# Decoding staged in PSUM, block sums of x on TensorE, and g read back earlier, in a fused attention and two-layer kernel

## The chip, the cores and the metric

One core of a Trainium2 chip runs the whole program. The metric is the device time of one execution in microseconds (us). Its engines run side by side, each through its own queue in order: TensorE (PE in the profile; PEld is its weight load), VectorE (DVE), ScalarE (ACT), GpSimd (POOL) and SyncE (SP), which here issues every DMA. An instruction that waits holds up all that stands behind it on its engine.

## The reference

Inputs q, k, v and g_norm are float32; the weights come as float64. Four batches of 576 tokens, 8 heads of 64.

```python
kv  = einsum('bhsd,bhse->bhde', k, v)
out = einsum('bhsd,bhde->bhse', q, kv)
x   = out / sqrt(mean(out*out, -1) + 1e-6) * g_norm      # -> 2304 x 512
g   = (x @ w_a) * (x @ w_b)                              # 2304 x 1536
y   = g @ w_out                                          # 2304 x 512
h   = y @ w_in                                           # 2304 x 1024
solu = h * softmax(h)
ln   = (solu - mean(solu)) / sqrt(var(solu) + 1e-6) * g_ln
return ln @ w_out2                                       # 2304 x 512
```

## The kernel before

**Attention.** For each batch, four pairs of heads: `att_kv` (L651, L655) forms kv of a pair from a tile `kv` in one of two buffers, so the load of the third pair waits until TensorE has used the first. `att_1` (L681) multiplies 128 tokens of q by kv for one tile of tokens, ScalarE squares (L707), VectorE reduces (L697), GpSimd takes the power (L709), VectorE scales (L710). `att_2` (L741) transposes the result into PSUM, ScalarE copies it scaled by g_norm (L761). There are 20 such tiles.

**Operands of the first product.** x @ w_a and x @ w_b are done as seven block products (`PROD`, P1 to P7) in place of eight; they need sums of blocks of x (`t_sums`, L720 to L728: three VectorE instructions per tile) and of the weights (`sums`, L489, also three). Each operand is kept as a high and a low part: ScalarE copies the high part (`pair_ops`, L733), VectorE or GpSimd subtracts it (`tt`, L266, printed as L269). x is cut into three groups of 288, 416 and 448 columns; groups 0 and 1 (12 tiles) are summed tile by tile, group 2 (8 tiles) in `third_group` once all tiles are there, in one chain of two steps.

**Weights.** They arrive as 64-bit words. `decode` turns a chunk of 128 x 512 into two float32 parts: ScalarE (L428), then five VectorE instructions (L431, L434, L440, L445, L449) on a scratch tile `u` and a tile `f` in SBUF. For each of twelve blocks f of w_a and w_b, two chunks are decoded, added (`gather`), summed (`sums`) and split into the operand `aw` (`make_w`); there is one stage buffer (`R_ST`) and two operand slots (`R_W`). The later weights (w_out, w_in, w_out2: 28 "late" chunks) are decoded beside the products; the twelve of w_out go to HBM (`lscw`) and are read back when x's place `a01` is free (`late_loads`, L974).

**Products.** A `Set` is one f with one group: seven products of 6 matmuls each (L865) on three PSUM banks, with copies by ScalarE (L883) and sums by VectorE (L896, L917, L924, L937) and GpSimd (L939). The result g goes to HBM (L947). All eight banks are shared.

**Second half.** `g_more` (L987) reads g back in pieces of 128 x 512 (L1004) and splits them (L1013, L269); `y_run` (L1041 to L1043) multiplies by w_out; `run_h` (L1083 to L1085, the helper `three`) by w_in; softmax and statistics follow on VectorE and ScalarE; `run_t` (L1158) transposes; `run_o` (again L1083) multiplies by w_out2.

**Order.** Nothing is scheduled by hand: `Order` keeps a planned time for each engine with prices such as `t_vec` and `t_pool`, and the code emits instructions in the order of that plan. `tt` picks VectorE or GpSimd by its planned end. A changed price therefore reorders much of the program. `FIRST` says how many chunks of weights may be loaded after how many loads of the attention. `lates`, `place` and `own` decide when late chunks are loaded.

Of the kernel before, what the change touches and what calls it, by code (L numbers as in the profile page):

```python
# [17 lines left out]
P = 128  # L18
# [46 lines left out]
NOP = 7  # L65
EARLY = 2
# [12 lines left out]
class Order:  # L79
# [48 lines left out]
    def load(self, nbytes):  # L128

        self.dma = max(self.dma, self.now + 0.7) + nbytes / 360e3  # L130
        return self.dma + 1.1
# [52 lines left out]
def t_pool(n):  # L184
    return 0.22 + n * 2.2e-3
# [7 lines left out]
def attention_moe_moe_kernel(ctx: ExitStack, tc, kv_in, kv_tail, q_in, g_norm, w1, w_in, w_out2, g_ln, out):  # L193
# [42 lines left out]
    ps_free = {i: 0.0 for i in range(8)}  # L236
# [49 lines left out]
    xs_ = [att.tile([P, H * D], F32, tag=f"x{i}", name=f"x{i}") for i in range(4)]  # L286

# [27 lines left out]
    FIRST = {0: 0, 3: 1, 5: 2, 12: 3, 14: 4, 28: 5, 30: 6}  # L315
    w_loads, l_loads = list(w_chunks), list(lates)
    n_load = [0, 0]
# [36 lines left out]
    def next_chunk(limit):  # L354
# [4 lines left out]
        for k in l_loads:  # L359
            if can(R_RAW, k) and (own() and left01[0] > 4 or place(k) is not None):  # L360
                l_loads.remove(k)
                return k
# [56 lines left out]
    def decode(k):  # L419
# [4 lines left out]
        ub, fb = u.bitcast(U32), f.bitcast(U32)  # L424

        def a():

            nc.scalar.activation(out=u, in_=w[:, :, 1].bitcast(F32), func=AF.Abs)  # L428

        def b1():  # L430
            nc.vector.tensor_scalar(out=u, in0=u, scalar1=WMIN, scalar2=WMAX, op0=ALU.max, op1=ALU.min)  # L431

        def b2():
            nc.vector.tensor_scalar(  # L434
                out=ub, in0=ub, scalar1=3, scalar2=0x3FFFFFF8, op0=ALU.logical_shift_left, op1=ALU.bitwise_and
            )

        def b3():

            nc.vector.scalar_tensor_tensor(  # L440
                out=fb, in0=w[:, :, 1], scalar=0xC0000000, in1=ub, op0=ALU.bitwise_and, op1=ALU.bitwise_or
            )

        def b4():
            nc.vector.tensor_scalar(out=ub, in0=fb, scalar1=0xFF800000, scalar2=None, op0=ALU.bitwise_and)  # L445

        def b5():

            nc.vector.scalar_tensor_tensor(  # L449
                out=u, in0=w[:, :, 0], scalar=2.0 ** -52, in1=u, op0=ALU.mult, op1=ALU.mult  # L450
# [13 lines left out]
        od.chain(  # L464
            [("A", 0.62, a), ("V", 0.5, b1), ("V", 0.5, b2), ("V", 0.75, b3), ("V", 0.5, b4), ("V", 0.75, b5),
             (None, 0, freed), (None, 0, last)],
            rank=rank_of(k), t=max(od.now, when),
        )
# [20 lines left out]
    def sums(f, st, t):  # L489
# [3 lines left out]
        def s32():  # L493
            nc.vector.tensor_tensor(
                out=s[:, 2:6:3], in0=s[:, 2:5:2], in1=s[:, 0:1].to_broadcast([P, 2, 256]), op=ALU.subtract)

        def ready(t):
# [47 lines left out]
    def store(k, f, u, su, t):  # L545

        what, x, y = k
        at = place(k)
        if at is None:
            at, d = l_pair[su - 2].bitcast(F32R), dr.tile([P, 2 * CH], F32, tag=f"lsc{what}{x}_{y}", name=f"lsc{what}{x}_{y}")  # L550
            lsc[k] = d
        else:
            d = None
        hi, lo = at[:, 0:CH], at[:, CH:2 * CH]
        if what == "o":
            g = gl_sb[:, x:x + 1]
            ops = [
                tt(CH, f, f, u, ALU.add),
                ("A", 0.7, lambda: nc.scalar.activation(out=hi, in_=f, func=AF.Copy, scale=g)),
                ("V", 0.7, lambda: nc.vector.scalar_tensor_tensor(  # L560
                    out=lo, in0=f, scalar=g, in1=hi.bitcast(F32), op0=ALU.mult, op1=ALU.subtract)),
            ]
        else:
            ops = [
                ("A", 0.6, lambda: nc.scalar.copy(out=hi, in_=f)),
                tt(CH, f, f, hi.bitcast(F32), ALU.subtract),
                tt(CH, lo, f, u, ALU.add),
# [783 lines left out]
```

## Time and profile before

| what | value |
|---|---|
| median of 3 runs (lowest to highest) | 774.54 us (773.36 to 777.3) |
| profiled execution, whole | 779.11 us |
| its span, first to last instruction | 777.1 us |
| TensorE busy | 712.5 us, 92% of the span |
| VectorE / ScalarE / GpSimd busy | 503.4 / 260.2 / 287.7 us |
| mean granted clock of TensorE | 0.971 |

The last chain of work is almost wholly TensorE's own. TensorE runs at two levels, 2.4 and 1.2 GHz; PEclk 1.00 is the higher one. Four stages can be told apart by the lines that TensorE runs: attention with the first two blocks f (to about 140 us), the products of f = 2 to 11 (to 384 us), the first part of y (to about 460 us), and y, h and the output together (to the end).

### The profile page before, as it was taken

What the parts mean: (1) busy time and instruction counts of PE and PEld (TensorE: products, weight loads), DVE (VectorE), ACT (ScalarE), POOL (GpSimd) and SP (SyncE); (2) the same over time, 40 slices, a digit from 0 to 9 for tenths busy, and PEclk for the clock granted to TensorE, in tenths of its full rate; (3) what the DMA queues carried; (4) which work ended last, traced back from release to release, by engine and by line L of the source; (5) the groups of instructions that cost most, each with busy time, mean ns of one, the idle gap of its engine ahead of it and who ended that gap; (6) DMA issues with size and microseconds to landing.
All of it is one profiled execution on the core that took longest, in us unless ns stands there. A gap on an engine that the chain in (4) does not pass through costs nothing. (4 is left out here: it accounts for less than half of the span.)

```text
span 777.1 us, 9816 instructions
## 1 busy us (share of the span) xinstructions
PE 712.5 (92%) x3664; PEld 622.4 (80%) x3664; DVE 503.4 (65%) x742; ACT 260.2 (33%) x444; POOL 287.7 (37%) x259
## 2 busy tenths in 40 slices
PE   5996887899989988989798899999999998999996
PEld 4785876889989988889676687888778887898885
DVE  2799877898999989993679999500642035315560
ACT  2564443334333333322334334322222222222221
POOL 1765632444463535532355754124212321122120
PEclk9898999999999999999989999999999999999998
DMA  7755003344444434523954531214002200120001
GB/s 255 285 185 185 16 23 104 144 154 143 146 148 168 164 109 158 198 78 133 407 176 163 178 125 50 55 41 122 1 14 82 89 14 14 38 65 15 14 14 41
DMA packets 36623, 87.68 MB, mean 113 GB/s; under 512 B 4448, under 2 KB 12384, under 8 KB 36576
## 3 DMA queue, kind: packets, MB, share of 16 engines
q1 hardware_dynamic: 36576, 87.05, 32.7%
q8 instruction: 29, 0.48, 0.2%
q14 instruction: 18, 0.15, 0.1%
HBM read 61.87 MB, written 25.17 MB: 112 GB/s over the span
## 5 line engine op out<-in xcount | busy, mean ns | idle before, releaser
L865 PE MATMUL ps<-a,aw 128*128 128x288 f32 (+2 forms) x1512 | 280.5, 345 | 22.6 <-DVE t L917 12.0
L865 PEld LDWEIGHTS ps<-a,aw 128*128 128x128 f32 x1512 | 260.6, 192 | 40.1 <-DVE t L917 15.4
L269 POOL TENSOR_TENSOR gy<-mx,gy 128x512 fp32r<-128x512 f32 (+1 forms) x46 | 53.8, 1180 | 96.0 <-ACT gy L1013 92.7
L939 POOL TENSOR_TENSOR gg<-gg,t 128x288 f32<-128x288 f32 (+2 forms) x36 | 47.7, 1324 | 82.4 <-DVE gg L937 72.0
L1042 PE MATMUL ps<-gy,a 128*128 128x512 f32 (+1 forms) x192 | 70.4, 366 | 3.8 <-POOL gy L269 2.2
L1083 PE MATMUL ps<-a,aw 128*128 128x512 f32 x171 | 68.9, 403 | 4.9 <-DVE aw L1168 4.7
L1041 PE MATMUL ps<-gy,a 128*128 128x512 f32 (+1 forms) x192 | 70.2, 366 | 0.0
L1043 PE MATMUL ps<-gy,a 128*128 128x512 f32 (+1 forms) x192 | 69.7, 363 | 0.0
L883 ACT COPY gg<-ps 128x288 f32<-128x288 f32 (+2 forms) x72 | 34.5, 479 | 100.1 <-PE ps L865 89.5
L1085 PE MATMUL ps<-a,aw 128*128 128x512 f32 x171 | 67.8, 396 | 0.0
L1084 PE MATMUL ps<-a,aw 128*128 128x512 f32 x171 | 67.7, 396 | 0.0
L269 POOL TENSOR_TENSOR mx<-f,u 128x512 f32<-128x512 f32 x23 | 33.0, 1434 | 68.2 <-DVE u L449 68.2
L1129 DVE TENSOR_REDUCE mx<-ps 128x1 f32<-128x1024 f32 x18 | 22.0, 1220 | 47.1 <-PE ps L1085 46.9
L1013 ACT CAST gy<-mx 128x512 fp32r<-128x512 f32 (+1 forms) x48 | 27.1, 566 | 58.6 <-DMA mx<-gd 35.6
L1042 PEld LDWEIGHTS ps<-gy,a 128*128 128x128 f32 x192 | 36.2, 189 | 11.7 <-POOL gy L269 4.3
L1168 DVE TENSOR_TENSOR aw<-ps,aw 128x1024 fp32r<-128x1024 f32 x13 | 15.9, 1222 | 45.5 <-ACT aw L1167 45.4
L1083 PEld LDWEIGHTS ps<-a,aw 128*128 128x128 f32 x171 | 32.9, 192 | 12.6 <-DVE aw L1168 5.2
L1083 PE MATMUL ps<-a 128*128 128x512 f32 (+1 forms) x106 | 40.8, 385 | 2.4 <-DVE a L1168 2.4
L709 POOL TENSOR_TENSOR r<-r,mhalf 128x8 f32<-128x8 f32 (+1 forms) x20 | 34.7, 1749 | 17.8 <-DVE r L698 17.7
L1041 PEld LDWEIGHTS ps<-gy,a 128*128 128x128 f32 x192 | 36.2, 189 | 5.6
L1043 PEld LDWEIGHTS ps<-gy,a 128*128 128x128 f32 x192 | 36.2, 189 | 5.4
L1084 PE MATMUL ps<-a 128*128 128x512 f32 (+1 forms) x106 | 40.5, 382 | 0.0
(121 smaller groups left out, 1279.3 us busy)
## 6 DMA issues: line engine op xcount, KB each, us to landing
raw<-in_w SPq DMA_DIRECT2D x24, 512.0 KB, 3.5
mx<-gd SPq DMA_DIRECT2D x48, 256.0 KB, 3.6
kv<-in_kv SPq DMA_DIRECT2D x16, 512.0 KB, 4.3
mx<-in_w SPq DMA_DIRECT2D x12, 512.0 KB, 3.4
lscw<-mx SPq DMA_DIRECT2D x12, 512.0 KB, 2.9
a<-lscw SPq DMA_DIRECT2D x12, 512.0 KB, 10.8
gd<-gg SPq DMA_DIRECT2D x12, 448.0 KB, 2.6
gd<-gg SPq DMA_DIRECT2D x12, 416.0 KB, 2.6
```

The source lines that it names most:

```text
L269: lambda e=e: e.tensor_tensor(out=out, in0=in0, in1=in1, op=op) for e in (nc.vector, nc.gpsimd)))
L709: ("G", 1.75, lambda: nc.gpsimd.tensor_tensor(out=r[0:n], in0=r[0:n], in1=mhalf[0:n], op=ALU.pow)),
L865: nc.tensor.matmul(o, lhsT=a[:, k], rhs=b[:, kt], start=first and kt == m == 0, stop=kt == 1 and m == 2, skip_group_check=not first,)
L883: od.chain([("A", t_act(s.n, True), lambda: nc.scalar.copy(out=dst(), in_=ps)), (None, 0, done)], t=t)
L939: ("G", t_pool(s.n), lambda: nc.gpsimd.tensor_tensor(out=d, in0=d, in1=t3, op=ALU.mult)),
L1013: ("A", t_act(n), lambda t=t, gh=gh: nc.scalar.copy(out=gh, in_=t)),
L1041: nc.tensor.matmul(o, lhsT=wh[:, s], rhs=gh, start=f == 0, stop=False)
L1042: nc.tensor.matmul(o, lhsT=wh[:, s], rhs=gl, start=False, stop=False)
L1043: nc.tensor.matmul(o, lhsT=wl[:, s], rhs=gh, start=False, stop=f == NF1 - 1)
L1083: nc.tensor.matmul(o, lhsT=ah, rhs=bh, start=first, stop=False)
L1084: nc.tensor.matmul(o, lhsT=ah, rhs=bl, start=False, stop=False)
L1085: nc.tensor.matmul(o, lhsT=al, rhs=bh, start=False, stop=last)
```

## The change

- The scratch tile of decoding lies in PSUM banks 6 and 7 (`v = pst[:, 6 + su]`) for chunks in the first two buffers; the sets and y have the other six banks until the last late chunk is decoded.
- For groups 0 and 1, TensorE forms the block sums: `x` as the stationary operand times a matrix `mix` of 0, 1 and -1, four matmuls per tile into a second bank. ScalarE writes the high parts straight from PSUM, VectorE the low parts, in three instructions. `t_sums` and the tile `xs` are gone for these 12 tiles.
- `third_group` runs its sums in two chains of two quarter steps.
- `sums` of the weights may go to GpSimd; prices of `tt`, `t_pool`, `load` and the decode steps are raised.
- `g_more` loads pieces of g without waiting for a place for the split; the reads of `lscw` come block by block; eleven late chunks, not twelve, are decoded beside the products.
- A late chunk's high part is copied before its last decode step. y takes its operand slot at the end of a block, not at its start. Batch 1's kv comes after all tiles of batch 0; `FIRST` loads weights later; while tiles of attention are left only one set is active.

```diff
-    ps_free = {i: 0.0 for i in range(8)}
+    ps_free = {i: 0.0 if i < 6 else INF for i in range(8)}
...
-        return ("VG", (t_vec(n), t_pool(n)), tuple(
+        return ("VG", (0.2 + n * 1.3e-3, t_pool(n)), tuple(
...
+    mix = {}
+    for n in (P, D):
+        c = n // 2
+        m1, m2 = (att.tile([P, 4, c], F32, tag=f"m{n}_{i}", name=f"m{n}_{i}") for i in range(2))
...
-    FIRST = {0: 0, 3: 1, 5: 2, 12: 3, 14: 4, 28: 5, 30: 6}
+    FIRST = {0: 0, 6: 1, 9: 2, 14: 3, 16: 4, 28: 5, 30: 6}
...
-        ub, fb = u.bitcast(U32), f.bitcast(U32)
+        v = pst[:, 6 + su] if su < 2 else u
+        vb, fb = v.bitcast(U32), f.bitcast(U32)
...
-            nc.vector.tensor_scalar(out=u, in0=u, scalar1=WMIN, scalar2=WMAX, op0=ALU.max, op1=ALU.min)
+            nc.vector.tensor_scalar(out=v, in0=v, scalar1=WMIN, scalar2=WMAX, op0=ALU.max, op1=ALU.min)
...
-            ("V", t_vec(256), lambda: nc.vector.tensor_tensor(out=s[:, 4], in0=s[:, 2], in1=s[:, 3], op=ALU.add)),
-            ("V", t_vec(512), s32),
-            ("V", t_vec(256), lambda: nc.vector.tensor_tensor(out=s[:, 6], in0=s[:, 1], in1=s[:, 5], op=ALU.subtract)),
+            tt(256, s[:, 4], s[:, 2], s[:, 3], ALU.add),
+            tt(512, s[:, 2:6:3], s[:, 2:5:2], s[:, 0:1].to_broadcast([P, 2, 256]), ALU.subtract),
+            tt(256, s[:, 6], s[:, 1], s[:, 5], ALU.subtract),
...
-            if 0 < i and b < B - 1:
+            if 0 < b < B - 1 and i:
                 front.append(("kv", b + 1, i - 1))
+        if not b:
+            front += [("kv", 1, p) for p in range(NP)]
...
+        for kt in range(2):
+            o = pt[:, kt * 4 * c:(kt + 1) * 4 * c]
+            for first, m in ((True, m1), (False, m2)):
+                p = kt if first else kt + 2
+                nc.tensor.matmul(o, lhsT=x[0:n, p * P:(p + 1) * P], rhs=m[0:n], start=first, stop=not first)
...
-            ops += t_sums(s, full[:, 8:16]) + pair_ops(hi, lo, full[:, 2:16]) + [(None, 0, done2)]
...
-                at = place(k)
+                at = place(k) if k[0] != "w" or k[1] < 2 or len(g_q) < len(YB) * NF1 and k[1] < y_next[1] + 6 else None
...
-        while g_q and R_GI.ok() and R_GP.ok():
+        while g_q and R_GI.ok():
...
-        if not now and order and len(sets) < ACTIVE:
+        if not now and order and len(sets) < (1 if att_left[0] else ACTIVE):
```

What this moves shows in the order of instructions at three places. The first is TensorE's queue at the first tiles of attention. `kv` and `tail` feed `att_kv`; `bd` with `q` is `att_1`; `ident` with `x` is the transpose of `att_2`; `m` is the new matrix. Before:

```order
L681 MATMUL ps<-bd_0_100,q_0_157 128x128
L681 MATMUL ps<-bd_1_102,q_1_159 128x128
L681 MATMUL ps<-bd_2_104,q_2_161 128x128
L681 MATMUL ps<-bd_3_106,q_3_163 128x128
L741 MATMUL ps<-ident,x_120 128x128 x4
L651 MATMUL ps<-kv_2_224 128x128 x4
L655 MATMUL ps<-tail_0_185 128x128
```

With the change:

```order
L723 MATMUL ps<-bd_0_100,q_0_176 128x128
L723 MATMUL ps<-bd_1_102,q_1_179 128x128
L723 MATMUL ps<-bd_2_104,q_2_181 128x128
L723 MATMUL ps<-bd_3_106,q_3_183 128x128
L785 MATMUL ps<-ident,x_120 128x2x64 x4
L809 MATMUL ps<-m_0_124,x_120 128x256
L809 MATMUL ps<-m_1_125,x_120 128x256
```

Behind the transposes now stand the new matmuls of the same tile (these two twice, then the next tile); the kv pairs of batch 1, which stood between the tiles of batch 0, come after them.

The second place is SP's queue where the products of groups 0 and 1 are done and those of group 2 still run. `a<-lscw` reads w_out back, `mx<-gd` reads g, `raw` is a chunk of weights. Before:

```order
L974 DMA a_81<-lscw_2_2621 128x1024
L974 DMA a_81<-lscw_2_2777 128x1024
L1004 DMA mx<-gd_82 128x512
L1004 DMA mx<-gd_83 128x512
L1004 DMA mx<-gd_84 128x512
L947 DMA gd_93<-gg_1_2840 128x2x416
L334 DMA raw_125<-in_w_out 128x512
```

With the change:

```order
L352 DMA raw_146<-in_w_out 128x512
L1036 DMA a_81<-lscw_2_1155 128x1024
L1036 DMA a_81<-lscw_2_1306 128x1024
L1062 DMA mx<-gd_82 128x512
L1062 DMA mx<-gd_83 128x512
L1062 DMA mx<-gd_84 128x512
L1036 DMA a_81<-lscw_2_1484 128x1024
```

The first three pieces of g stood behind all twelve reads of w_out; now they stand behind two of them.

The third place is TensorE's queue at the last tile: `ident,mx` is the transpose of `run_t`, and what follows it is `run_o`. Before:

```order
L1084 MATMUL ps<-aw,a_81 128x512
L1085 MATMUL ps<-aw,a_81 128x512
L1158 MATMUL ps<-ident,mx 128x128 x8
L1083 MATMUL ps<-a_81 128x256
L1084 MATMUL ps<-a_81 128x256
```

With the change:

```order
L1153 MATMUL ps<-aw,a_81 128x512
L1154 MATMUL ps<-aw,a_81 128x512
L1227 MATMUL ps<-ident,mx 128x128 x16
L1152 MATMUL ps<-a_81 128x512
L1153 MATMUL ps<-a_81 128x512
```

The output product of the last tile (in halves of 256) followed its own transpose at once; now two transposes stand together, and the output product of the tile before (512 wide) stands between the last transpose and its product.

## Rows read from the trace of the kernel before

**Rows 1.** Busy time by stretch: start:end, length, then engines, clock, DMA, GB/s.
```profile
0.00:50.00 50.00, 37.93 (x225) 32.00 (x226) 30.94 (x70) 23.09 (x51) 22.47 (x21) 0.93 0.75 263
50.00:104.00 54.00, 45.07 (x309) 41.35 (x309) 44.67 (x84) 29.40 (x55) 29.68 (x18) 0.94 0.26 90
104.00:140.00 36.00, 27.18 (x123) 23.56 (x121) 28.55 (x38) 11.38 (x16) 12.96 (x7) 0.95 0.23 81
140.00:345.00 205.00, 194.47 (x1078) 183.89 (x1078) 187.35 (x292) 73.83 (x134) 93.04 (x65) 0.98 0.42 146
345.00:384.00 39.00, 35.58 (x181) 32.70 (x180) 23.18 (x36) 10.79 (x19) 10.77 (x8) 0.96 0.64 243
384.00:460.00 76.00, 66.58 (x270) 52.05 (x271) 63.99 (x75) 29.98 (x49) 46.06 (x31) 0.96 0.52 184
460.00:777.00 317.00, 305.69 (x1484) 256.85 (x1482) 124.66 (x152) 81.75 (x123) 72.68 (x111) 0.98 0.15 42
```

**Rows 2.** TensorE's waits: line, waited for, us in total, times, longest.
```profile
PE ps L865 <- DVE t L917: 12.0, 10, 2.4
...
PE ps L741 <- DVE xs L724: 5.7, 1, 5.7
PE ps L1083 <- DVE aw L1168: 4.7, 2, 2.4
...
PE ps L865 <- DVE aw L269: 3.1, 2, 2.6
PE ps L1041 <- ACT a L1013: 3.0, 1, 3.0
PE ps L865 <- ACT t L883: 2.8, 3, 1.5
...
PE ps L865 <- ACT a L733: 2.4, 1, 2.4
PE ps L1083 <- DVE a L1168: 2.4, 1, 2.4
```

**Rows 3.** Timeline of TensorE in attention: start, us, line, count of records.
```profile
28.88 1.06 PE L651 MATMUL ps<-kv 128*128 128x128 f32 x8
29.87 0.48 PE L655 MATMUL ps<-tail 64*128 64x128 f32 x2
```

**Rows 4.** DMA issues: tile, count, KB each, median us to landing.
```profile
kv<-in_kv SPq DMA_DIRECT2D x16, 512.0 KB, 4.3
...
q<-in_q SPq DMA_DIRECT2D x16, 288.0 KB, 5.4
```

**Rows 5.** Timelines of GpSimd and VectorE at 55 us.
```profile
55.67 2.20 POOL L269 TENSOR_TENSOR a<-xs,a 128x896 fp32r<-128x896 f32 x1 [2.82 <-ACT a L733]
...
55.83 2.33 DVE L431 TENSOR_SCALAR u<-u 128x512 f32<-128x512 f32 x1
```

**Rows 6.** Single lines of VectorE: duration ns min/median/max, first and last start.
```profile
L431 DVE TENSOR_SCALAR u<-u x40: 413/420/2327, 11.5 to 470.1; 128x512 f32<-128x512 f32 x40
...
L440 DVE SCALAR_TENSOR_TENSOR f<-raw,u x40: 674/692/1787, 12.5 to 474.4; 128x512 uint32<-128x512 uint32 x40
...
L710 DVE TENSOR_TENSOR x<-ps,r x20: 672/683/693, 25.4 to 98.5; 128x512 f32<-128x512 f32 x16, 64x512 f32<-64x512 f32 x4
```

**Rows 7.** VectorE's groups at 170 to 340 us: count, busy us, mean ns, idle.
```profile
L494 DVE TENSOR_TENSOR mx<-mx 128x512 f32<-128x512 f32 x7 | 6.7, 963 | 0.1
...
L504 DVE TENSOR_TENSOR mx<-mx 128x256 f32<-128x256 f32 x7 | 6.6, 938 | 0.0
...
L502 DVE TENSOR_TENSOR mx<-mx 128x256 f32<-128x256 f32 x7 | 4.0, 569 | 0.0
```

**Rows 8.** Timeline of TensorE in the products, between two waits.
```profile
250.09 22.39 PE L865 MATMUL ps<-a,aw 128*128 128x416 f32 x126 [0.54 <-DVE t L917]
```

**Rows 9.** Timeline of SP's DMA queue ahead of y.
```profile
363.85 9.53 SPq L974 DMA_DIRECT2D a<-lscw  x12
...
375.66 2.86 SPq L1004 DMA_DIRECT2D mx<-gd  x3
```

**Rows 10.** A stretch behind one of the three L1083 waits, columns as Rows 1.
```profile
565.00:570.00 5.00, 5.00 (x16) 3.99 (x17) 3.18 (x5) 0.00 (x0) 1.51 (x3) 0.69 0.00 0
```

More of the change, by code (lines that the diff above doesn't have):

```diff
@@ L359, in next_chunk @@
         for k in l_loads:
-            if can(R_RAW, k) and (own() and left01[0] > 4 or place(k) is not None):
+            if can(R_RAW, k) and (own() and n_late[0] < IN_AB or place(k) is not None):
                 l_loads.remove(k)
+                n_late[0] += 1
                 return k
@@ L462, in last @@
                 gather(k, f, u, su, t)
[L464 to L468, printed above, removed]
+        ops = [("A", 0.67, a), ("V", 0.68, b1), ("V", 0.68, b2), ("V", 0.7, b3), ("V", 0.6, b4), ("V", 0.7, b5),
+               (None, 0, freed), (None, 0, last)]
+        if is_late(k) and k[0] != "o":
+            ops[5:5] = [(None, 0, lambda t: upper(k, f, su, t))]
+        od.chain(ops, rank=rank_of(k), t=max(od.now, when))
     def gather(k, f, u, su, t):
@@ L563, in store @@
         else:
[L564 to L567, printed above, removed]
-            ]
+            ops = [tt(CH, lo, f, u, ALU.add)]
         def done(t):
@@ L745, in att_2, with scaled @@
         rank = 1 + b
-        if g == 2:
-            sxs = None
-            s = g2s[:, :, c0:c0 + c]
-        else:
-            sxs = R_XS.take()
-            full = att.tile([P, 16 * 64], F32, tag="xs", name=f"xs{b}_{t}", bufs=2)
-            full = full[:, 0:16 * c].rearrange("p (r c) -> p r c", c=c)
-            s = full[:, 0:8]
+        if g < 2:
+            R_PA.take()
+        def scaled(out, src, m):
+            return ("A", t_act(m, True, True), lambda: nc.scalar.activation(
+                out=out, in_=src, func=AF.Copy, scale=gn[:, 0:1]))
@@ L774, in att_2 @@
-        od.chain(ops, rank=rank, t=od.now + 0.25)
+        if g == 2:
+            R_X.give(sx)
+            od.chain([scaled(g2s[:, :, c0:c0 + c], rows, 8 * c), ps_done(bank), (None, 0, done),
+                      (None, 0, lambda t: one_left(g, t))], rank=rank, t=od.now + 0.25)
+            return
+        bank2, pt = ps_tile()
+        m1, m2 = mix[n]
+        for kt in range(2):
[3 more added lines that the diff above has]
+                nc.tensor.matmul(o, lhsT=x[0:n, p * P:(p + 1) * P], rhs=m[0:n], start=first, stop=not first)
@@ new lines, in att_2, with done2 @@
+        R_X.give(sx)
+        hi, lo = (y[:, :, c0:c0 + c] for y in x_ops(g))
+        left = [2]
+        def done2(when):
+            R_PA.give(1)
+            left[0] -= 1
+            if not left[0]:
+                one_left(g, when)
+        sums = pt[:, 0:8 * c].rearrange("c (k r t) -> c k r t", k=2, r=4)
+        for bk, src, h, l, m, dt in (
+            (bank, rows[:, 2:8], hi[:, 0:6], lo[:, 0:6], 6 * c, 0.25),
+            (bank2, None, hi[:, 6:14], lo[:, 6:14], 8 * c, 1.2),
+        ):
+            if src is None:
+                h, l = (y.rearrange("p (r k) c -> p k r c", k=2) for y in (h, l))
+                low = [("V", t_vec(m // 2, True), lambda k=k, h=h, l=l: nc.vector.scalar_tensor_tensor(
+                    out=l[:, k], in0=sums[:, k], scalar=gn[:, 0:1], in1=h[:, k].bitcast(F32),
+                    op0=ALU.mult, op1=ALU.subtract)) for k in range(2)]
+                src = sums
+            else:
+                low = [("V", t_vec(m, True), lambda src=src, h=h, l=l: nc.vector.scalar_tensor_tensor(
+                    out=l, in0=src, scalar=gn[:, 0:1], in1=h.bitcast(F32), op0=ALU.mult, op1=ALU.subtract))]
+            od.chain([scaled(h, src, m)] + low + [ps_done(bk), (None, 0, done2)], rank=rank, t=od.now + dt)
@@ L790, in third_group @@
         slot = R_ST.take()
-        full = wst.rearrange("p (r c) -> p r c", c=GN[2] // 2)
-        step = GN[2] // 2
-        left, left_b = [4], [2]
+        left, left_b = [6], [2]
         def done(t):
@@ L1026, in y_can @@
         if f == 0:
-            t = max(t, ps_ready2(2)) if R_Y.ok() else INF
+            t = max(t, ps_ready2(2))
+        if f == NF1 - 1 and not R_Y.ok():
+            return INF
         return t
@@ L1044, in y_run @@
         end = od.now + 12 * t_mm(n)
-        od.chain([(None, 0, lambda t: R_GP.give(sg)), (None, 0, lambda t: g_more())], t=end)
+        od.chain([(None, 0, lambda t: R_GP.give(sg)), (None, 0, lambda t: g_split())], t=end)
         y_next[1] += 1
```

142 lines of the change are left out of this document (82 added, 60 removed).

## The prediction

> **What bounds the kernel now.** I read the busy time by stretch first, then TensorE's list of waits, then single rows. TensorE is busy 92% of the span, so a gain has to come out of its gaps and its slow clock, and every matmul added costs unless it fills a gap. The stretches [rows 1] show where the gaps are. Up to 140 us TensorE is busy 37.9 of 50, 45.1 of 54 and 27.2 of 36 us: 29.8 us idle, and the granted clock of 0.93, 0.94 and 0.95 says that about 3.5 + 3.2 + 1.8 = 8.5 us more went at the lower level. From 140 to 345 us it idles 10.5 us (clock 0.98, 4 us), while VectorE is busy 187 of 205 us: two engines are nearly full. From 345 to 384 us 3.4 us are idle, from 384 to 460 us 9.4 us (clock 0.96, 3 us). After that only 11.3 us are idle, 4 of them behind the last matmul.
>
> The list of waits [rows 2] names VectorE for most of it. The largest, 12.0 us in ten waits, is the sum in line 917: it waits in VectorE's queue behind decoding. In the attention stage 5.7 us (sums of x), 2.4 us (split of group 2) and 2.6 us (split of weights) are the long ones. The last stage has three waits of 2.4 us each for line 1168, each where a tile's output product follows its transpose at once.
>
> Why VectorE is so full shows in two rows: GpSimd's subtraction takes 2.20 us from 55.67 us on, and a step of decoding beside it takes 2.33 us [rows 5], against a median of 0.42 us [rows 6]. Line 440 ranges from 0.67 to 1.79 us. Line 710, which reads PSUM, ran 20 times between 0.67 and 0.69 us beside the same GpSimd work [rows 6]. So operands in SBUF are stretched by GpSimd and those in PSUM were not.
>
> **The change part by part.** I sum against the profiled execution, 779.1 us (span 777.1 and 2 us around it), which is 4.6 us over the median.
>
> *Attention and the first two weight blocks (0 to 140 us).* The four added matmuls per tile are 256 columns wide for ten tiles and 128 for two. Eight records in line 651 are four matmuls of 128 columns in 1.06 us [rows 3], 0.265 us each. A 256-column one lies between that and double, 0.53 us; I take 0.47, near the upper end, since the columns are streamed. 40 x 0.47 + 8 x 0.265 = 21 us (12.7 to 23.3) on the bounding engine. What they replace, per tile, is three sums on VectorE, a subtraction of the low part on VectorE or GpSimd and a copy on ScalarE; three low parts from PSUM come to VectorE, at line 710's rate (0.683 us for 512 columns) 0.5 + 0.34 + 0.34 us. The clash with GpSimd leaves this path, and the 5.7 us wait for `xs` has no cause left. Of the 29.8 us idle and 8.5 us slow clock, the waits for VectorE and for group 2 and the slow clock behind them are about 21 us; I take 18 as filled, since the third group's two halves run on two engines at once and TensorE has products left meanwhile.
>
> Two new waits come with the order. kv has two buffers, so batch 1's third pair is loaded only after TensorE has used the first; in between stands one pair, (1.06 + 0.48) = 1.5 us, and a load lands after 4.3 us [rows 3, 4]: 2.8 us of wait. Behind that load on SP stand the fourth pair, a chunk of weights and all q of batch 1 (5.4 us to land [rows 4]), so the first tile of batch 1 waits about as long: 5.6 us together. Before, tiles stood between those pairs. The weights' chunks are issued behind q; the first set needs all of batch 0's tiles anyway, which hides that. One chunk fewer stands ahead of batch 0's q: 0.5 MB at 263 GB/s [rows 1] is 2 us gained. Sum: 21 - 18 + 5.6 - 2 = +6 us, between -4 (matmuls at 0.27, all 21 filled) and +14 (12 filled).
>
> *Products of f = 2 to 11.* Decoding a chunk on VectorE is three steps of 0.42 and two of 0.69 us undisturbed, 2.64; in PSUM I bound the step from both sides by 0.42 and 0.69 and take 0.69 (line 710's row is PSUM), 3.45 us. Disturbed, the stage pays more than 2.64: the sums of weights in the same stage average 0.96, 0.94 and 0.57 us [rows 7], 2.47 per f. Of these 36 instructions 29 now stand on GpSimd. At 2.20 us for 896 columns [rows 5] it needs 2.5 us per f for them and is busy only 93 of 205 us. So VectorE loses some 2 us per f out of 21 and gains slack; the waits for line 917 should fall. What is there to win is the stage's 10.5 + 4 us and, to 384 us, 3.4 + 1.6. Against it: with six banks and one set active at some ends of f, P4 follows P7 at once in two more places (about 0.65 us each, as in two of the three waits for line 883 [rows 2]), and the weights' chain (decode, gather, sums, copy, split, through one stage buffer) has the sums on the slower engine. TensorE's floor per f is 22.4 us for 126 matmuls [rows 8]; before, an f took about 23.2 us. I take 8 us of the 19.5, -18 to +3.
>
> The Trainium skill, "VectorE: DVE Perf Modes", section "Why PSUM operands drop a tier", says that a float32 instruction with a PSUM operand runs one element per cycle. That speaks against the change: three of the five steps lose their double rate. "SBUF — State Buffer", section "Who interferes with whom", says that an instruction with at most one SBUF input outside those modes doesn't contend with GpSimd. By the first alone the products gain 4 us, by both 8.
>
> *Start of y.* The three pieces of g stood behind 9.5 us of w_out reads [rows 9]; now behind two of twelve. The 3.0 us wait [rows 2] and the slow clock behind it (3 us) go; the later 6.4 us of waits are for splits, whose loads now run ahead: 12.4 at most. The other ten reads are asked for six blocks ahead of use (12 matmuls of 0.24 us a block, worked out below, is 17 us), which hides them. Two costs: y's second block needs a pair of banks of the first block while 6 and 7 hold decoding (0 to 2.6 us, I take 1), and sixteen late chunks cost VectorE 0.8 us more each undisturbed where it is already busy 64 of 76 us (I take 3). Net -8 (-12 to 0).
>
> *The last stage.* In the new order another product stands between every transpose and its output product. The waits of 2.4 + 2.4 + 2.4 us go, and the slow clock behind each: 0.69, 0.66 and 0.66 over 5 us (the first is [rows 10]), 5 us. Left: the last transpose now has only one output product and a transpose ahead (24 matmuls of 512 columns at 22.39/126 x 512/384 = 0.24 us each, and 0.9 us), and the product behind it waits for its own drain, up to 2.4 less 0.9 us; I take 2. -10 (-12 to -7).
>
> Part with one answer: the matrices of 0 and 1 are made while TensorE waits for the first kv.
>
> **The rivals.** *Attention costs nothing and the products reach their floor.* VectorE's relief decides both: 0 - 15 - 11 - 11 = -37, 742 us in the trace, 737 as a median. For it: VectorE is named in most waits. Against: a wait for DMA isn't VectorE's.
>
> *The weights' chain binds.* GpSimd's sums take away what PSUM gives: products 0, attention +10, y -7, end -10, that is -7: 767. For it: VectorE's other work on SBUF is still stretched by a busier GpSimd [rows 5].
>
> *Slower.* The same chain gets longer than the products' time: with period T per f in place of 23.2 us the nine f that wait for it cost 9 x (T - 23.2); the other terms give 12 us (6 - 8 - 10), so it decides from T = 24.5 on, and at T = 26 the end is 13 us over: 787. GpSimd takes over 29 instructions that are each slower than on VectorE, and a set's multiplication (L939) queues with them.
>
> *It doesn't do what it says: PSUM only slows decoding.* Steps at 0.69 us and the two that read `raw` still stretched: products -4, y 0 since VectorE is full there (64 + 16 x 0.8 = 77 of 76 us), end -10, attention +6: -8, 766. The page on perf modes, cited above, is the rule by which this would come; the trace bears it out as far as the 0.42 against 0.69 us goes, and speaks against the stretching.
>
> **How the numbers follow.** 6 - 8 - 8 - 10 = -20: 759.1 in the profiled execution, less 4.6 gives a median of 754 us, -2.6%. Chances: the forecast 0.48 (744 to 764); attention free and products at the floor 0.18; chain binds 0.18 (760 to 775); slower 0.08; PSUM only slows 0.08. The range of 8 in 10 runs from 737 to 771: half of the best rival lies below, most of the slower case and a part of the chain's above. A measurement here tells about 0.5% (3.9 us) from no change: faster 0.86 (all but a third of the chain's case and the slower one), same 0.08, slower 0.06.
>
> **What would show it.** Attention: products of f = 2 begin near 146 us (140 before), VectorE less busy ahead of it, a wait for kv's third pair of batch 1 near 38 us. Products: VectorE's decode steps within 0.67 to 0.70 us, waits for the c22 sum under 8 us, and a period of f below 23 us. y: no wait over 1 us at its first piece and a clock of 1.00 there. End: no wait for a drain behind a transpose but at the last tile. I am wrong if GpSimd appears as releaser of the weights' split, if f = 2 begins past 155 us, or if decode steps in PSUM vary.

## The result and the profile after

The changed kernel took 756.55 us (median of 4 runs, 755.03 to 757.83), the kernel before 775.92 us beside it (773.36 to 778.2): a ratio of 0.975, 95% interval 0.971 to 0.979. The prediction was 754.0 (737 to 771). The profiled execution took 757.83 us, its span is 755.9.

Three landmarks divide both executions: where the products of f = 2 begin, where the products end, and the end. These are the stretches between them, the last one cut once more at 480 us. Columns: stretch, its length, busy time of each engine with the number of instructions, granted clock, share of DMA, GB/s. Before:

```profile
core 0: us, PE busy (x) PEld busy (x) DVE busy (x) ACT busy (x) POOL busy (x), PEclk, DMA share, GB/s
0.00:140.36 140.36, 110.18 (x655) 96.90 (x655) 104.53 (x192) 63.88 (x120) 65.11 (x45) 0.94 0.43 149
140.36:383.65 243.29, 230.05 (x1258) 216.59 (x1258) 209.82 (x325) 84.62 (x153) 103.81 (x72) 0.98 0.45 162
383.65:480.00 96.35, 86.48 (x361) 68.45 (x361) 83.53 (x102) 38.76 (x62) 56.74 (x41) 0.96 0.45 160
480.00:777.00 297.00, 285.78 (x1394) 240.45 (x1392) 105.47 (x126) 72.97 (x110) 61.99 (x101) 0.98 0.15 40
```

After:

```profile
0.00:147.61 147.61, 131.69 (x750) 117.60 (x751) 100.15 (x198) 62.21 (x123) 68.01 (x53) 0.95 0.40 143
147.61:383.41 235.80, 226.15 (x1259) 213.94 (x1259) 200.73 (x296) 82.74 (x152) 122.29 (x95) 0.99 0.45 156
383.41:480.00 96.59, 91.87 (x404) 74.66 (x403) 81.92 (x115) 41.05 (x66) 53.76 (x46) 1.00 0.54 183
480.00:756.00 276.00, 270.28 (x1350) 228.82 (x1348) 103.12 (x120) 70.44 (x105) 58.67 (x96) 1.00 0.15 40
```

The first stretch is 7.25 us longer: TensorE has 21.5 us more to do there, and its idle time falls from 30.2 to 15.9 us. The products are 7.5 us shorter. From their end to the end of the span it was 393.45 us and is now 372.5, which is 21 us less, half of it idle time (21 to 10 us), half of it clock. From TensorE's list of waits after:

```profile
PE ps L926 <- POOL aw L270: 7.9, 3, 3.8
PE ps L693 <- DMA kv<-in_kv: 5.5, 2, 4.1
...
PE ps L723 <- DMA q<-in_q: 1.9, 2, 1.0
PE ps L1111 <- POOL a L270: 1.8, 2, 0.9
PE ps L1110 <- DVE aw L1136: 1.4, 1, 1.4
...
PE ps L1152 <- DVE a L1237: 1.3, 1, 1.3
...
PE ps L926 <- DVE t L978: 0.6, 1, 0.6
```

The last row is the sum that took 12.0 us in [rows 2]. The three waits of 2.4 us behind drains have shrunk to one of 1.3. At the head of the list stands a new one: the split of the weights on GpSimd. The decode steps with scratch in PSUM, by form (busy time, mean ns):

```profile
L451 DVE TENSOR_SCALAR ps<-ps 128x512 f32<-128x512 f32 x41 | 27.6, 688 | 18.2 <-ACT ps L448 18.2
L454 DVE TENSOR_SCALAR ps<-ps 128x512 uint32<-128x512 uint32 x41 | 27.9, 691 | 0.4
L460 DVE SCALAR_TENSOR_TENSOR f<-raw,ps 128x512 uint32<-128x512 uint32 x41 | 27.7, 678 | 0.7
L465 DVE TENSOR_SCALAR ps<-f 128x512 uint32<-128x512 uint32 x41 | 28.0, 686 | 0.4
L469 DVE SCALAR_TENSOR_TENSOR u<-raw,ps 128x512 f32<-128x512 uint32 x41 | 27.7, 679 | 0.4
```

None of these is under 0.63 or over 0.70 us, where [rows 6] had 0.41 to 2.33. Eleven of the 52 chunks use another buffer, whose scratch stays in SBUF, and there a step varies as before in the same execution (shortest, median and longest in ns, then first and last start):

```profile
L465 DVE TENSOR_SCALAR mx<-mx x11: 414/742/2652, 145.2 to 325.5; 128x512 uint32<-128x512 uint32 x11
```

### The profile page after: what moved, and what is told of

It is laid out like the page before. It is cut to its first block, busy times and chain, and to the rows that moved or that the text cites. A ratio compares the mean times of both kernels' runs of the same rounds, so it can differ in the third digit from the quotient of the medians.

```text
span 755.9 us, 10032 instructions
## 1 busy us (share of the span) xinstructions
PE 720.0 (95%) x3760; PEld 635.0 (84%) x3760; DVE 485.9 (64%) x726; ACT 256.4 (34%) x446; POOL 302.7 (40%) x287
## 4 chain that ended last, share of the span: by engine, by line
PE 79%; DVE 9%; DMA 3%; POOL 3%; issue 2%; ACT 2%; SPq 0%; POOLq 0%; DVEq 0%; ACTq 0%
PE ps L926 26%; PE ps L1152 9%; PE ps L1154 9%; PE ps L1153 9%; PE ps L1110 5%; PE ps L1111 5%; PE ps L1112 5%; PE ps L809 3%; PE ps L723 3%; PE ps L693 2%; PE ps L1227 2%; PE ps L785 1%; POOL mx L270 1%; DVE mx L460 1%; DMA kv<-in_kv 1%
## 5 line engine op out<-in xcount | busy, mean ns | idle before, releaser
L926 PE MATMUL ps<-a,aw 128*128 128x288 f32 (+2 forms) x1512 | 274.3, 341 | 14.7 <-POOL aw L270 7.9
L926 PEld LDWEIGHTS ps<-a,aw 128*128 128x128 f32 x1512 | 256.6, 189 | 30.2 <-POOL aw L270 8.6
L270 POOL TENSOR_TENSOR gy<-mx,gy 128x512 fp32r<-128x512 f32 (+1 forms) x43 | 50.0, 1163 | 96.4 <-ACT gy L1081 93.0
L1152 PE MATMUL ps<-a,aw 128*128 128x512 f32 (+1 forms) x178 | 67.9, 381 | 0.0
L1153 PE MATMUL ps<-a,aw 128*128 128x512 f32 (+1 forms) x178 | 67.8, 381 | 0.0
L1154 PE MATMUL ps<-a,aw 128*128 128x512 f32 (+1 forms) x178 | 67.8, 381 | 0.0
L1000 POOL TENSOR_TENSOR gg<-gg,t 128x288 f32<-128x288 f32 (+2 forms) x36 | 41.4, 1150 | 58.0 <-DVE gg L998 57.9
L270 POOL TENSOR_TENSOR mx<-mx 128x512 f32<-128x512 f32 (+2 forms) x45 | 57.7, 1287 | 6.5 <-DVE mx L270 2.0
L1237 DVE TENSOR_TENSOR aw<-ps,aw 128x1024 fp32r<-128x1024 f32 x13 | 15.9, 1224 | 44.3 <-ACT aw L1236 44.2
L1199 ACT ACTIVATE mx<-ps,mx 128x1024 f32<-128x1024 f32 x18 | 20.1, 1118 | 69.0 <-DVE mx L1198 69.0
L1152 PE MATMUL ps<-a 128*128 128x512 f32 x99 | 38.8, 392 | 1.3 <-DVE a L1237 1.3
```

Source lines behind the costliest of these rows:

```text
L926: nc.tensor.matmul(o, lhsT=a[:, k], rhs=b[:, kt], start=first and kt == m == 0, stop=kt == 1 and m == 2, skip_group_check=not first,)
L1000: ("G", t_pool(s.n), lambda: nc.gpsimd.tensor_tensor(out=d, in0=d, in1=t3, op=ALU.mult)),
L1152: nc.tensor.matmul(o, lhsT=ah, rhs=bh, start=first, stop=False)
L1153: nc.tensor.matmul(o, lhsT=ah, rhs=bl, start=False, stop=False)
L1154: nc.tensor.matmul(o, lhsT=al, rhs=bh, start=False, stop=last)
```

## The experiments

All twelve in one table, each with its median, its ratio to the kernel before beside it, and the three stretches of its profiled execution (to f = 2; products; from the products' end to the end). "After" and "before" stand for the whole change and none of it. The stretches are those of one execution each, and that one lay up to 3.2 us from the median (3.2 above it before, 1.3 above it after, 2.3 below it with scratch in SBUF), so a difference of 2 or 3 us between two kernels can be chance.

| kernel | median us | ratio (95%) | first | products | rest |
|---|---|---|---|---|---|
| before | 775.9 | 1 | 140.4 | 243.3 | 393.5 |
| after | 756.55 | 0.975 (0.971 to 0.979) | 147.6 | 235.8 | 372.5 |
| after, scratch in SBUF | 774.08 | 0.998 (0.995 to 1.001) | 145.3 | 244.2 | 380.4 |
| the same with eight banks | 766.65 | 0.988 (0.982 to 0.994) | 147.2 | 243.7 | 376.2 |
| after, slot taken early | 781.44 | 1.005 (1.002 to 1.008) | 144.6 | 238.1 | 396.1 |
| after, g late | 771.47 | 0.992 (0.989 to 0.995) | 146.7 | 238.3 | 385.3 |
| after, third group in one chain | 759.07 | 0.979 (0.974 to 0.984) | 147.2 | 239.1 | 372.6 |
| after, half of the block sums | 749.8 | 0.967 (0.962 to 0.973) | 136.2 | 238.8 | 372.6 |
| after, weight sums on VectorE | 754.96 | 0.974 (0.968 to 0.980) | 146.1 | 233.9 | 372.6 |
| after, weight split on VectorE | 755.17 | 0.974 (0.969 to 0.979) | 145.4 | 234.2 | 372.8 |
| after, third buffer for kv | 764.8 | 0.984 (0.979 to 0.989) | 146.7 | 244.7 | 373.1 |
| before with PSUM alone | 783.25 | 1.009 (1.006 to 1.011) | 142.7 | 238.7 | 397.6 |
| before with late slot alone | 770.1 | 0.993 (0.991 to 0.995) | 138.3 | 243.2 | 386.4 |
| before with both | 764.16 | 0.986 (0.980 to 0.992) | 142.0 | 238.6 | 380.2 |

**Scratch in SBUF, banks still closed.**

```diff
-        v = pst[:, 6 + su] if su < 2 else u
+        v = u
```

> The third group's decode scratch goes back to SBUF, banks 6 and 7 stay closed to the products, nothing else is changed, so every engine has the instructions of the changed kernel in the same order. Theory (the prediction's: in SBUF the decode step is stretched by GpSimd, in PSUM it isn't): decode steps of 256 columns spread again from 0.42 us to over 2 us, with means at or over the 0.68 to 0.69 us that they take in PSUM, and 759 to 766 us, 3 to 9 over the changed kernel. Rival (reading PSUM is what costs VectorE its speed, and the rest of the change carries the gain): the mean step falls clearly under 0.68 us and the time is 748 to 755 us.

(The edit puts back the scratch of the first two decode buffers, whatever the group, and the steps have 512 columns.) It took 774.08 us: nearly the whole gain is gone, about twice the most that the theory gave. The rival is out. The steps of decoding, in the same order of instructions as after:

```profile
L451 DVE TENSOR_SCALAR u<-u 128x512 f32<-128x512 f32 x41 | 27.2, 678 | 19.7 <-ACT u L448 19.7
L454 DVE TENSOR_SCALAR u<-u 128x512 uint32<-128x512 uint32 x41 | 28.3, 700 | 0.4
L460 DVE SCALAR_TENSOR_TENSOR f<-raw,u 128x512 uint32<-128x512 uint32 x41 | 39.0, 954 | 0.7
L465 DVE TENSOR_SCALAR u<-f 128x512 uint32<-128x512 uint32 x41 | 23.1, 565 | 0.4
L469 DVE SCALAR_TENSOR_TENSOR u<-raw,u 128x512 f32<-128x512 uint32 x41 | 30.6, 750 | 0.4
```

Three of the five have a median of 0.42 us, as the first of them has in [rows 6], and yet two of those three have about the mean that they have in PSUM, since single ones last up to 1.5 us. The five sum to 148.2 us here and 138.9 in PSUM; VectorE's whole busy time is 498.7 and 485.9 us. About as much is won on the other side: GpSimd is busy 314.8 us here and 302.7 after. One of its groups, after and then here:

```profile
L270 POOL TENSOR_TENSOR f<-f,a 128x512 f32<-128x512 f32 x9 | 11.7, 1295 | 16.9 <-ACT a L583 12.0 <-DVE ps L465 4.8
```

```profile
L270 POOL TENSOR_TENSOR f<-f,a 128x512 f32<-128x512 f32 x9 | 14.2, 1576 | 21.0 <-ACT a L583 18.2 <-DVE u L465 2.8
```

The stretching goes both ways, and PSUM takes it off these steps of both engines. I had priced VectorE's side alone. Decoding also ends earlier with the slower step. The last of the five, after and then here:

```profile
L469 DVE SCALAR_TENSOR_TENSOR u<-raw,ps x41: 633/678/689, 21.4 to 482.7; 128x512 f32<-128x512 uint32 x41
L469 DVE SCALAR_TENSOR_TENSOR u<-raw,u x41: 640/683/1773, 21.3 to 496.1; 128x512 f32<-128x512 uint32 x41
```

By stretch the products lose 8.4 us and the rest 7.9, while the first stretch is 2.3 shorter. In the products TensorE's idle time is 13.65 against 9.65 us, and its busy time is 4.4 us longer for the same matmuls, which is clock (0.97 against 0.99). In the rest the waits for the split of one piece of g (3.6 in place of 0.9 us), which on GpSimd stands behind late decoding, and for closed banks (2.7 and 3.0 us in place of 1.4) add up.

**The same with all eight banks open.**

```diff
-    ps_free = {i: 0.0 if i < 6 else INF for i in range(8)}
+    ps_free = {i: 0.0 for i in range(8)}
...
-        v = pst[:, 6 + su] if su < 2 else u
+        v = u
...
-                ps_free[6] = ps_free[7] = t
+                pass
```

> As the run with scratch in SBUF, and all eight banks are open to the products again, so the order may shift a little. Theory: as there, less what the two closed banks cost; that is the wait of 1.4 us of y's second block, so 757 to 766 us, within 3 us of the run with six banks. Rival (the closed banks are what the PSUM staging really costs): 5 us or more under the run with six banks, and below the changed kernel.

It took 766.65 us, 7.4 less than with six banks, which is more than the theory's 3 and what the rival asked for, but still 10 above the changed kernel, which it did not. The two profiled executions lie only 2.8 us apart, so the traces account for a part of the 7.4. With SBUF scratch the two banks matter, since decoding ends late and they stay closed until then: the waits of 2.7 and 3.0 us are gone here. After, where decoding ends earlier, the closed banks cost the one wait of 1.4 us shown above.

**Slot taken early.** y takes its operand slot at the start of a block, as before.

```diff
-            t = max(t, ps_ready2(2))
-        if f == NF1 - 1 and not R_Y.ok():
-            return INF
+            t = max(t, ps_ready2(2)) if R_Y.ok() else INF
...
+            y_op[j] = (R_Y.take(),)
...
-            slot = R_Y.take()
+            slot = y_op[j][0]
```

> y takes its operand slot at the start of a block again, as in the kernel before, and not at its end. Theory (the late taking is what lets the products of the last blocks of y run past the drains, and with it the three waits of 2.4 us behind drains went): they come back and the time is 761 to 769 us. Rival (the waits at the end went because the new plan orders the drains otherwise, and the slot is not what it turns on): the end is unchanged and the time is 755 to 758 us.

781.44 us: all of the gain is gone and more, above the theory's 769. Four rows of TensorE's timeline say why (start, us, instruction, idle time before it and its releaser):

```profile
482.01 0.77 PE L1151 MATMUL ps<-a,aw 128*128 128x512 f32 x1 [11.59 <-DVE u L469]
...
566.99 0.50 PE L1151 MATMUL ps<-a,aw 128*128 128x512 f32 x1 [2.36 <-DVE aw L1236]
...
649.37 0.50 PE L1151 MATMUL ps<-a,aw 128*128 128x512 f32 x1 [2.36 <-DVE aw L1236]
...
758.09 0.50 PE L1151 MATMUL ps<-a 128*128 128x512 f32 x1 [2.36 <-DVE a L1236]
```

The first is the first output product. The program puts it behind the decoding of the last late chunk and gives it one of decoding's two banks. The releaser, a decode step that starts at 481.2 us, shares nothing with it but that bank, so the wait is for a bank of decoding's. The program has nothing else for TensorE there: y's next block may not start, since both operand slots are held. Behind the wait the clock is 0.86 from 475 to 520 us. In the changed kernel the last decode step is as late (482.7 us), but there stand 72 matmuls of y's next block behind the first transpose, some 16 us of work (0.227 us each, by their starts). The waits behind drains come back too, with no block of y put between.

**g late.** The first pieces of g are read behind w_out again. The edit undoes three things at once: the early reads of g, the reads of `lscw` block by block, and the limit of eleven late chunks.

```diff
-IN_AB = 11
+IN_AB = 99
...
-            if can(R_RAW, k) and (own() and n_late[0] < IN_AB or place(k) is not None):
+            if can(R_RAW, k) and (own() and left01[0] > 4 or place(k) is not None):
...
-                at = place(k) if k[0] != "w" or k[1] < 2 or len(g_q) < len(YB) * NF1 and k[1] < y_next[1] + 6 else None
+                at = place(k)
...
-        while g_q and R_GI.ok():
+        while g_q and R_GI.ok() and R_GP.ok() and len(g_in) == 0 and (g_q[0][0] == 0 or gy):
```

> The first pieces of g are read behind all of w_out's reads again, and the split of g is queued as before; the rest is the changed kernel. Theory (the early pieces are what took the wait and the half clock from the start of y): y begins with a wait of 2 to 4 us and at a clock under 0.9, and the time is 760 to 765 us. Rival (the faster decoding alone had made the chain of w_out early enough): no wait over 1 us at y's first piece and 755 to 758 us.

Neither came. y starts well, with a wait of 0.69 us and a clock of 1.00 from 384 to 430 us, so the early pieces are not what took the wait from its start. But the time is 771.47 us: the rest is 12.8 us longer, and it is lost late:

```profile
710.38 1.09 PE L1227 MATMUL ps<-ident,mx 128*128 128x128 f32 x8 [1.10 <-DVE mx L1203]
...
742.04 1.09 PE L1227 MATMUL ps<-ident,mx 128*128 128x128 f32 x8 [1.98 <-DVE mx L1203]
746.60 0.79 PE L1152 MATMUL ps<-a 128*128 128x512 f32 x1 [3.46 <-DVE a L1237]
758.11 0.39 PE L1152 MATMUL ps<-a 128*128 128x256 f32 x1 [2.36 <-DVE a L1237]
```

Here y's last matmuls start at 691.8 us (684.1 after), and in TensorE's queue the last four transposes have 24, 96 and 24 matmuls between them, where after the last six, of which the first two and the last two stand together, have 72, 72 and 48. From 745 us on the clock is 0.78. So the three count together, through y's blocks being done sooner and the order of the end that follows; which of them does it isn't separated.

**Half of the block sums.** Of each pair of new matmuls the second is left out, so the combined blocks of x lack their second signed part.

```diff
-            for first, m in ((True, m1), (False, m2)):
+            for first, m in ((True, m1),):
...
-                nc.tensor.matmul(o, lhsT=x[0:n, p * P:(p + 1) * P], rhs=m[0:n], start=first, stop=not first)
+                nc.tensor.matmul(o, lhsT=x[0:n, p * P:(p + 1) * P], rhs=m[0:n], start=True, stop=True)
```

> Of the sums of x's blocks on TensorE the second matmul of each pair is left out, so the combined blocks hold only the first of their two signed parts (this part of the computation is left out): 8 pairs of 128x256 matmuls less one half. As the trace of the changed kernel has them (0.47 us each at 256 columns, 0.265 at 128) half of the added 21 us is gone. Theory (in the attention TensorE is the bound, so the added matmuls count in full): f=2 begins 7 to 11 us earlier and the time is 746 to 750 us. Rival (the first blocks of weights, not TensorE, set when f=2 begins): f=2 begins 0 to 3 us earlier and the time is 753 to 757 us.

f = 2 begins 11.4 us earlier for 10.5 us of matmuls less, so the rival is out. That they count in full is in part luck: the clock from 40 to 50 us is 0.83 here and 0.50 in the changed kernel, so TensorE's busy time falls by 15.9 us, while its idle time rises by 4.5. Then 3.0 us are given back in the products, and the median falls by 6.75.

**Third group in one chain of two steps.**

```diff
-        left, left_b = [6], [2]
+        left, left_b = [4], [2]
...
-        step = GN[2] // 4
-        for h in range(2):
+        step = GN[2] // 2
+        for h in range(1):
```

> The third group's sums in one chain of two steps in place of two chains; the rest is the changed kernel, and the order of the last stage is the same. Theory (two chains let two engines work at once on the group that is needed last): operands of the third group come 2 to 4 us later, f=2 begins up to 4 us later, 757 to 761 us. Rival (in the changed kernel the group is ready with time to spare): f=2 begins within 1 us of 147.6 and the time is 755 to 758 us.

759.07 us (757.75 to 760.91), hardly to be told from 756.55. f = 2 begins at 147.23 us, so two chains gain nothing there. Of the 3.3 us in the products 2.6 are busy time, which is clock: 0.86 against 0.93 from 140 to 165 us and 0.93 against 1.00 from 340 to 365 us, behind waits of the same length (3.66 and 3.19 us here, 3.83 and 3.22 after).

**Weight sums on VectorE, and weight split on VectorE.** Two runs, each with one of them.

```diff
-            tt(256, s[:, 4], s[:, 2], s[:, 3], ALU.add),
+            ('V', 0.53, lambda: nc.vector.tensor_tensor(out=s[:, 4], in0=s[:, 2], in1=s[:, 3], op=ALU.add)),
...
-                    tt(n, lo[:, s], x, hi[:, s].bitcast(F32), ALU.subtract),
+                    ("V", t_vec(n), lambda s=s, x=x, hi=hi, lo=lo: nc.vector.tensor_tensor(out=lo[:, s], in0=x, in1=hi[:, s].bitcast(F32), op=ALU.subtract)),
```

(The other two sums are written the same way.)

> The three kinds of weight sums are put on VectorE alone (in the changed kernel GpSimd takes most of them); their order against the rest is left to the plan. Theory (GpSimd's slow sums, not VectorE, are what makes weight operands late): no wait of TensorE for a GpSimd split or sum, 750 to 755 us. Rival (VectorE, busy for 0.91 of the products, has no room for them): TensorE waits for VectorE in the products, f rises over 23 us, and the time is 757 to 768 us.

> The split of the combined weights' low part is always put on VectorE; in the changed kernel three of TensorE's waits, 7.9 us in sum (3.83, 3.22 and 0.83), end with that split on GpSimd. Theory (GpSimd is late for it, VectorE would not be): the three waits shrink to under 3 us and the time is 749 to 754 us. Rival (the sums before the split are late on either engine, so only the last link is shorter, and VectorE's queue is as full): the waits stay over 6 us in sum, 755 to 760 us.

754.96 us (754.32 to 756.5) and 755.17 us (754.25 to 757.62): both a little under the changed kernel, with ranges that overlap. So GpSimd's share of the sums gains nothing here. With the sums on VectorE the time lies where the theory had it, but its condition did not come: the waits for GpSimd's split are 9.2 us in sum. With the split on VectorE the wait stays, under another name:

```profile
PE ps L926 <- DVE aw L549: 8.6, 3, 4.3
```

The chain ahead of it is what is late. GpSimd in the changed kernel, ahead of the wait that ends at 147.61 us:

```profile
138.53 2.55 POOL L270 TENSOR_TENSOR mx<-f,u 128x512 f32<-128x512 f32 x2 [6.42 <-DVE u L469]
141.15 0.81 POOL L270 TENSOR_TENSOR mx<-mx 128x256 f32<-128x256 f32 x1
141.97 1.29 POOL L1000 TENSOR_TENSOR gg<-gg,t 128x448 f32<-128x448 f32 x1
143.89 0.72 POOL L270 TENSOR_TENSOR mx<-mx 128x256 f32<-128x256 f32 x1 [0.62 <-DVE mx L270]
144.57 1.58 POOL L1000 TENSOR_TENSOR gg<-gg,t 128x448 f32<-128x448 f32 x1
146.11 1.45 POOL L270 TENSOR_TENSOR aw<-mx,aw 128x512 fp32r<-128x512 f32 x1
```

From the last decode step (138.5 us) to the operand it is 9 us, one instruction after the other, with two multiplications of other sets in between. No single one of them makes up the wait.

**Third buffer for kv.**

```diff
-    R_KV, R_TAIL, R_Q, R_RAW = Ring(2), Ring(1), Ring(8), Slots(3)
+    R_KV, R_TAIL, R_Q, R_RAW = Ring(3), Ring(1), Ring(8), Slots(3)
```

(and `bufs=3` for the tile)

> A third buffer for the pairs of k and v, so that the third pair of the second batch is read without waiting for the first to be used. In the changed kernel TensorE waits 1.5 us for it at 39.75 us and 4.1 us at the start, and its clock is 0.50 of full from 40 to 50 us, which costs some 5 us. Theory (the wait and the half clock behind it go together): the clock of 40 to 50 us is over 0.9, f=2 begins 4 to 6 us earlier, and the time is 750 to 753 us. Rival (the clock falls there for the loosely filled attention as such): the wait goes, the clock stays near 0.5, and the time is 755 to 757 us.

The wait of 1.5 us at 39.75 us goes, and 8 us are lost: 764.8 us. The clock from 40 to 50 us is 0.66 after three short waits for q (0.50 in the changed kernel), so that wait isn't its whole cause; what is stays open. The loss lies in the products, 8.9 us. The plan has moved work between VectorE and GpSimd (497.8 and 292.6 us busy, 485.9 and 302.7 after), and the wait for f = 11's weights is 5.7 in place of 3.2 us.

**The two large parts alone, in the kernel before.** First PSUM staging with its prices and closed banks:

```diff
+        v = pst[:, 6 + su] if su < 2 else u
...
-    ps_free = {i: 0.0 for i in range(8)}
+    ps_free = {i: 0.0 if i < 6 else INF for i in range(8)}
...
-            [("A", 0.62, a), ("V", 0.5, b1), ("V", 0.5, b2), ("V", 0.75, b3), ("V", 0.5, b4), ("V", 0.75, b5),
+            [("A", 0.67, a), ("V", 0.68, b1), ("V", 0.68, b2), ("V", 0.7, b3), ("V", 0.6, b4), ("V", 0.7, b5),
```

> The kernel before with one part of the change alone: the decode scratch of its first two buffers in banks 6 and 7, those banks closed to the products, and the plan's prices of the decode steps set as in the changed kernel. With the scratch put back in SBUF the changed kernel took 774.1 us, 18 over the changed kernel, more than the 3 to 9 expected. Theory now (staging in PSUM is worth 10 to 18 us by itself, because it takes the clash with GpSimd off both engines): 758 to 766 us. Rival (it is worth that much only in the changed kernel, whose plan was fitted to it, and the other parts would be worth as much alone): 768 to 778 us.

Neither theory nor rival: 783.25 us, slower than before. The products are 4.6 us shorter, but the first stretch is 2.3 and the rest 4.2 longer, with this in it:

```profile
482.84 0.77 PE L1086 MATMUL ps<-a,aw 128*128 128x512 f32 x1 [9.13 <-DVE u L450]
```

It is the wait that the early slot made in the changed kernel: the first output product on a bank of decoding's. It ends with the last decode step on that bank; the last step of all starts later, at 486.5 us. So the slot alone, and then both:

```diff
-            t = max(t, ps_ready2(2)) if R_Y.ok() else INF
+            t = max(t, ps_ready2(2))
+        if f == NF1 - 1 and not R_Y.ok():
+            return INF
...
-            y_op[j] = (R_Y.take(),)
...
-            slot = y_op[j][0]
+            slot = R_Y.take()
```

> The kernel before with the late taking of y's operand slot alone. Taking it early again in the changed kernel brought back four waits of 2.36 us behind drains and a wait of 11.6 us for the decoding of w_out, 23.5 us from the start of y on. In the kernel before w_out isn't waited for, so only the drains can be won. Theory (the slot frees the order of the last stage): two of the three waits of 2.36 us go with the slow clock behind them, the one at the end stays, 766 to 771 us against 777. Rival (the slot is worth nothing without the rest): 774 to 779 us.

> The kernel before with two parts: decoding staged in PSUM (with the two banks closed) and the late taking of y's slot. PSUM alone took 783 us, with a wait of 9.1 us for w_out's decoding at 482.8 us and three of 2.36 us. Theory (the two parts need each other: PSUM makes the products shorter and w_out later, and the slot gives TensorE blocks of y to do until w_out is there): the 9.1 us wait goes with 5 us of slow clock behind it, as do two of the waits behind drains with theirs, and the time is 758 to 765 us, under the sum of the two parts alone. Rival (their effects just add up): PSUM's +5 to +8 and the slot's own gain, 771 to 777 us.

The slot alone: 770.1 us, as the theory had it, and of the three waits behind drains one is left. Both: 764.16 us, as the theory had it too; the wait of 9.13 us is gone, and the products are again 4.6 us shorter than with the slot alone. The ratios are 1.009 and 0.993 alone, which would multiply to 1.001, and 0.986 together.

## Why the prediction was right, and where it was not

**The sum.** By stretch it was 6 - 8 - 18 = -20, and the traces say 7.25 - 7.5 - 21.0 = -21.2. The terms came out; several of the reasons behind them did not. The median fell by 19.4 us. The step from trace to median, -4.6, was too large: the profiled execution lay 3.2 us over the median of the four runs of the kernel before, and 1.3 over that of the changed one.

**Attention, +6: right in the price of the matmuls, in part luck in the rest.** The 256-column matmul was taken at 0.47 us, and eight records, four matmuls, last 1.89 us:

```profile
25.84 1.89 PE L809 MATMUL ps<-m,x 128*128 128x256 f32 x8
```

TensorE's busy time rises by 21.5 us where 21 were summed, and 14.3 us of gaps are filled where 18 less 5.6 of new waits plus 2 made 14.4. But the 18 counted on slow clock as well, and of that hardly any was won: the clock of the stretch is 0.94 before and 0.95 after. The new waits came smaller, kv's at 39.75 us with 1.5 in place of 2.8 us and all waits for q with 1.9; in their place 5 us went where the sum had no term, at half clock behind the wait for kv (stretch, length, TensorE's busy time, its clock, DMA share and GB/s):

```profile
40.00:45.00 5.00, 5.00 (x24) 0.50 1.00 365
45.00:50.00 5.00, 5.00 (x22) 0.50 0.93 354
```

That the third group's two halves do the filling is wrong: one chain does as well.

**Products, -8: right in size, half of the reason wrong.** The forecast put the gain on two things, decoding freed from the clash and sums moved to GpSimd. The first carries all of it in the changed kernel, 8.4 us; in the kernel before it is 4.6. The second, undone, left the products no longer (233.9 us). I also called GpSimd as releaser of the weights' split a sign that I was wrong. It appeared, 7.9 us of it, and it didn't overturn the sum.

The Trainium skill, "VectorE: DVE Perf Modes", section "Why PSUM operands drop a tier", caps a float32 instruction with a PSUM operand at the single rate. The trace agrees for the three one-input steps: 0.69 us against a median of 0.42 in SBUF. In this kernel the tier is not the price that counts, since the mean in SBUF is 0.57 to 0.70 us for the same steps.

**Rest, -18 for -21: right in size, cause not named.** I wrote that in the new order another product stands between transpose and output product, and read this off the order. What makes that order is the late slot. Undone it costs 23.6 us here, and alone it brings 7.0 (393.5 to 386.4). The term for the start of y rested on g's early pieces; with them late, y starts as well, and their worth, up to 12.8 us together with what else that run undid, lies in the tail. The 3 us for slower decoding at the start of y had the wrong sign in the changed kernel: with scratch in SBUF the last decode step starts at 496.1 us, in PSUM at 482.7. What PSUM does cost is the bank that the first output product waits for, 9.1 and 11.6 us where the slot was taken early; with the late slot TensorE had other work.

**Adding up.** I summed the parts as independent. They aren't: from before to the slot, to slot and PSUM, to the whole the rest is 393.5, 386.4, 380.2 and 372.5 us, but PSUM without the slot makes it 397.6. With this PSUM alone would have been forecast too fast, as my expectation for that run was (758 to 766, and 783 measured).

**The rivals.** "PSUM only slows decoding" is out: in PSUM it takes less of VectorE in sum. "The weights' chain binds" names the longest wait that is left, but the products fell all the same: ten f take 235.8 us, 23.6 each, against 24.3 each before by the same count. The 23.2 that I took for the kernel before was too low, so the 24.5 from which the sign would have turned is 25.6 by this count. Below 23, as I wrote, the period isn't: 9.65 us idle and a clock of 0.99 stand between it and the floor of 22.4 [rows 8].

**What stays open.** Which part took the wait of 3 us from the start of y: with the slot and PSUM alone 2.9 us of it are still there, at the low part of the first piece, and with g late it is gone, so as far as these runs tell it is one of the remaining parts. Whether the block sums on TensorE pay at all: the whole without them wasn't run, and against the kernel with slot and PSUM the changed one is 5.6 us longer to f = 2, 2.8 shorter in the products and 7.7 in the rest. The new order of kv, `FIRST` and the single active set weren't run alone either. Of the variants that compute everything none is faster than the changed kernel by more than its runs spread.

## What to carry to other kernels

Where two engines stretch each other's work on a shared memory, count both sides: moving one engine's scratch to the other memory may pay although some of its steps get slower undisturbed. Before crediting or dropping a part of a change, run it alone and run the whole without it; a part that makes another engine wait, as PSUM's banks did here, can be worth its price only with the part that gives the waiting engine other work. A resource taken when a block is finished, and not when it is begun, can be that part.

## What the runs showed of the hardware

VectorE's decode steps beside GpSimd's work took 0.63 to 0.70 us with scratch in PSUM and up to 1.8 us with scratch in SBUF. GpSimd is slowed as well: nine of its subtractions took 1.295 us each with that scratch in PSUM and 1.576 with it in SBUF, and all its work 302.7 and 314.8 us. And TensorE's clock was not told by the length of the wait ahead of it: around a wait of 3.2 us the granted clock of the same stretch, 340 to 365 us, was 1.00 in one kernel and 0.93 in another, and it stood at 0.50 for 10 us where the wait before was 1.5 us.
